# Gated linear attention with a soft mixture of experts: four batches side by side, half blocks through the state, the carry on TensorE, and a new order

## The chip, the core and the metric

The kernel runs on one core of a Trainium2 chip. Five engines run it, each with a queue of its own: TensorE (PE, matrix products, with weight loads listed as PEld), VectorE (DVE), ScalarE (ACT), GpSimd (POOL) and SyncE (SP), which here issues DMAs. Products land in PSUM, eight banks of 512 fp32 values on each of 128 partitions; everything else works in SBUF. The metric is the device time of the program in microseconds.

## The reference

Inputs are q, k, v, a_re, a_im of 4 batches, 8 heads, 768 tokens and 48 channels; a_re is uniform on 0.85 to 0.95, a_im normal with standard deviation 0.1. The attention is a complex decay of a state; its result is the input of a soft mixture of 8 experts with 4 slots each.

```python
mag = np.sqrt(a_re * a_re + a_im * a_im)
scale = np.minimum(mag, 0.999) / (mag + 1e-06)
a_re_n, a_im_n = (a_re * scale, a_im * scale)
for t in range(S):
    new_re = ar * S_re - ai * S_im
    new_im = ar * S_im + ai * S_re
    S_re, S_im = (new_re + kv, new_im)
    y[:, :, t] = np.einsum('bhd,bhde->bhe', q[:, :, t], S_re)
x = y.transpose(0, 2, 1, 3).reshape(B * S, H * D)
logits = x @ phi
d = softmax over tokens of logits; slot_input = d.T @ x
h = np.maximum(slot_input[e] @ w1[e], 0.0); slot_out[e] = h @ w2[e]
out = softmax over slots of logits @ slot_out
```

## The kernel before

Tokens are taken in blocks of 128 (`g`), 24 of them, batch after batch: a block's state comes from the block before it of the same batch. Three blocks form a unit `u`; there are eight units. `_polar` is the fast path. For a group of blocks `gates` takes the logarithm of the decay's size and the ratio a_im/a_re, and `arctan` its angle. `phase` sums angles along the tokens with a triangular product on PE (`up`); the sum so far of the batch is added to one row of the block beforehand on VectorE (L640), then the sum is rounded to whole turns and the rest kept (L646, L648), and sine and cosine are taken on ScalarE (L653, L658). `expo` does the same for the decay (`lp`) and copies the block's last row into `rrow` with DMAs that ScalarE issues (L679); `decay` turns those rows. `mults` multiplies q and k by the decay on GpSimd (L694) and by sine and cosine on VectorE (L703), which gives `hat`; `xpose` turns it (PE L715, ScalarE L718), `score` forms the 128x128 scores of a head and masks them (PE L723, VectorE L727), `attend` adds scores times v and the state's part into `yb` (L748, L750), `delta` carries the state on (PE L761, VectorE L766, L768), and `xform` turns the result back (L773, copied by ScalarE, L776). `_Moe.logits` and `slots` take a unit's three blocks into running softmax sums, `merge` ends these, `hidden` and `experts` apply the weights, and `combine` forms the results of a block at a time and scales them with `rc`.

The order of all this is written out by hand in `ORDER`: each name runs a task's next step, and `_InOrder` holds every engine to the order in which the steps were traced. SP's loads stand in it too: seven weight chunks (`w0` to `w6`) at the start, three more along the way, and two groups of them near the end (`w12`, `w11`), where pools are given up (`swap`, `swap_wk`).

In PSUM a pool `ps2` has four buffers for turned tiles, scores and results (tag `tr`) and two for the rest (tag `lu`); `yb` and `db` have one bank each.

The fast path holds only where the decay behaves. `gates` therefore keeps the largest (a_im/a_re)² and the smallest a_re of each group, L908 to L919 compare them and others with bounds, L940 counts the partitions on which all is well, and L942 writes `bad`. After `_polar` the kernel reads it and, where it is over zero, runs `_stepwise`: the recurrence token by token on VectorE, in 48 rounds of 16 tokens, each with loads into single buffers, and the mixture after it, without overlap:

```python
rv = nc.values_load(bad)
with tc.If(rv > 0):
    with ExitStack() as st:
        _stepwise(st, tc, cst, phi_sb, dict(q=q, k=k, v=v, a_re=a_re, a_im=a_im), w1, w2, out)
```

Of the kernel before, what the change touches and what calls it, by code (L numbers as in the profile page):

```python
# [25 lines left out]
UB = 3  # L26
NU = NG // UB
# [21 lines left out]
TAU_MAX = 1.5  # L49
AR_MIN = 33.0 / 64.0  # L50
# [28 lines left out]

class _Moe:  # L80


# [42 lines left out]
    def slots(self, u, xs):  # L125
# [35 lines left out]
        nc.vector.reciprocal(out=self.rc[:, u, :].unsqueeze(2), in_=cs)

    def merge(self):
# [101 lines left out]
    def weights(self, er, us, j):  # L265
# [4 lines left out]
        yield from self.parts(er(us, j), ep, self.low[0])  # L270
# [5 lines left out]
    def combine(self, er, sr, skip, os_tile, out):  # L276

        nc, w = self.nc, out.shape[-1]
        for u in range(NU):
            os_ = os_tile(u)[:, 0 : UB * w].rearrange("p (j d) -> p j d", j=UB)  # L280
            for j in range(UB):
                o = self.ps.tile([P, skip + w], F32, name="o", tag="tr", bufs=NTR)
                nc.tensor.matmul(out=o, lhsT=er(u, j), rhs=sr, start=True, stop=True)  # L283
                if (UB * u + j) % 2:
                    nc.scalar.activation(out=os_[:, j], in_=o[:, skip:], func=AF.Copy, scale=self.rc[:, u, j : j + 1])
                else:
                    nc.vector.tensor_scalar(out=os_[:, j], in0=o[:, skip:], scalar1=self.rc[:, u, j : j + 1], scalar2=None, op0=ALU.mult)
                if u == 0:
                    nc.sync.dma_start(out=out[u][:, j], in_=os_[:, j])
                yield  # L290
            if u:
                nc.sync.dma_start(out=out[u], in_=os_)

# [3 lines left out]
    L0 lq0 w0 la0 w1 w2 w3 w4 w5 lv0 w6 g0 g0 wu1 g0 g0 wu2 g0 wu0 g0 wu3 g0 g1 g0 g0 g1 e0 g1 e0 g1 e0 e0 m0 T0 g1 t0 t1 p0 p0  # L297
    m0 p0 p0 p1 p0 L1 p1 m0 p1 x2 g1 x0 g1 p2 g1 p2 x0 g1 x2 p2 e1 g2 e2 la1 m0 g2 m0 g2 x1 x3 e1 g2 D0 e1 e1 D0 x1 x3 g2 c0 e2
    e2 c1 T1 c0 m1 c1 a0 e2 p1 a0 t2 p1 p1 p3 p2 p2 p3 m1 p2 L2 m1 x6 x4 p3 m2 x5 x4 x7 x6 d0 x5 d0 D0 x7 lq1 c2 p4 g2 c3 a0 g2
    p4 D1 c2 g2 D1 c3 a1 D1 g2 a1 D1 e3 m2 a1 e3 m2 x8 e3 x10 x8 p4 x9 x10 e3 x9 p5 e4 g3 e5 e4 e4 x11 m3 p5 x11 e4 D2 g3 p5 la2  # L300
    D2 g3 f0 D2 c4 m4 e5 e5 c5 c4 e5 T2 a2 c5 p3 p3 g3 a2 p3 p4 lv1 p4 d1 g3 f1 p4 a2 l0 p5 p5 m5 p5 l0 L3 d1 l0 l0 lq2 s0 s0 m3
    s0 g3 m3 f0 f1 g3 x13 x12 x14 s0 g3 x15 D3 x12 D3 g3 x14 x13 D2 x15 e6 m4 c6 e6 m4 e6 c7 e6 c6 x17 c7 x18 x17 D3 x16 m6 g4
    a3 x16 x18 a3 g4 D3 m5 e7 g4 x19 m5 e8 x19 g4 D4 a3 e7 D4 e7 e7 c8 g4 e8 e8 e8 c9 T3 c8 x22 c9 m7 t3 x21 D4 x20 x20 p6 x22
    m8 a4 x21 p6 a4 p6 p7 lq3 t4 p6 p7 D4 p6 x23 p7 c10 x23 c11 p8 p7 a4 p7 c10 p8 p7 c11 a5 la3 p8 a5 p9 m6 lv2 a5 m6 p8 x24
    x26 x24 p8 x25 m7 x26 x27 p8 l1 m7 L4 p9 l1 x25 D5 p9 x27 D5 g4 d2 c12 g4 c13 x29 d2 p10 g4 x28 p10 x28 g4 x29 c12 e9 p10
    x30 a6 x30 D5 e9 e10 p11 e9 c13 e9 e10 m8 e10 a6 e10 p11 m8 a6 e11 p11 m9 x31 la4 f2 x31 g5 D6 f2 D6 m10 g5 s0 f3 s0 g5 c14
    s0 f3 c15 c14 e11 e11 x32 c15 e11 T4 x33 D6 x34 D6 a7 x32 g5 x34 a7 p9 x33 p9 g5 p9 x35 D7 x35 m9 D7 t5 l1 m9 a7 p12 p10 p10
    l1 f4 m11 p10 f5 f4 p12 d3 f5 c16 d3 D7 p12 lq4 c17 p11 p11 c16 p11 x36 c17 L5 x37 p13 x38 a8 m10 s1 x36 s1 m10 s1 x38 a8
    x37 s1 D7 lv3 s1 a8 g5 p13 s1 l2 g5 x39 D8 x39 l2 s1 g5 D8 p13 c18 c19 c18 x40 c19 x42 x40 g5 x41 x42 x43 x41 x43 m11 e12
    e13 m11 e12 e12 a9 D8 e12 e13 D8 e13 a9 e13 p14 g6 p14 m12 a9 e14 p14 g6 D9 la5 D9 m13 g6 l2 l2 c20 s2 x44 s2 c20 c21 x44 D9  # L310
    e14 x46 c21 a10 x46 D9 e14 g6 T5 s2 a10 g6 e14 x45 x47 x45 s2 f6 x47 p12 f7 p12 m14 d4 f8 f6 d4 f7 c22 a10 t6 c23 c22 lq5
    p13 p13 a11 c23 p13 p15 f8 a11 m12 p14 p14 lv4 s2 m12 p14 x48 L6 s2 x50 s2 x49 m13 p15 x48 x50 x51 m13 x49 D10 x51 p15 D10
    a11 g6 l3 c24 g6 c25 l3 g6 c24 x54 x52 c25 x53 x52 g6 a12 x54 a12 D10 e15 a12 m14 x55 e15 e16 m14 e15 e15 x53 e17 p16 x55 g7
    D11 e16 e16 D11 e16 m15 p16 g7 D11 c26 g7 c27 c26 m16 e17 x58 e17 c27 x57 T6 a13 g7 e17 p15 a13 p15 g7 p15 x56 a13 l3 D12
    x56 l3 m17 x58 D12 t7 p16 x59 f9 p16 p16 lq6 d5 p16 d5 p17 f9 m15 x57 p17 x59 p18 m15 la6 f10 p18 f11 f10 f12 f11 p17 c28
    p18 f12 c29 p17 p17 c28 p17 x62 p19 L7 x61 c29 x60 D11 p19 s3 x63 x60 s3 D12 s3 x62 a14 s3 x61 D12 x63 m16 a14 m16 lv5 D13
    a14 p19 g7 D13 s3 g7 l4 c30 s3 g7 l4 s3 x64 c31 g7 x64 x66 c30 e18 x66 c31 x65 D13 e19 x65 m17 x67 a15 m17 x67 e18 D13 e18
    a15 e18 p20 p18 g8 p20 a15 e19 D14 e19 m18 p20 D14 e19 g8 e20 D14 g8 l4 l4 c32 w7 m19 c33 s4 e20 s4 c32 x69 e20 c33 T7 s4
    x68 s4 x70 g8 p18 a16 x69 x68 g8 a16 x70 e20 p19 x71 p19 m18 f13 p19 f14 x71 m18 c34 f13 f14 m20 a16 x72 c34 c35 x72 p20 x74
    p20 w8 s4 x74 p20 x73 s4 x75 L8 s4 d6 D15 d6 c35 x73 D15 D14 x75 a17 D15 g8 a17 g8 lv6 f15 m19 f16 g8 c36 m19 f15 c37 a17 g8  # L320
    f16 x77 x78 x77 c36 e21 c37 x76 a18 x76 m20 a18 x78 m20 D16 a18 e21 D16 e21 e21 e22 D16 e23 D16 e22 e22 x79 l5 x79 m21 e22
    e23 D17 l5 e23 T8 D17 l5 l5 f17 m22 e23 f18 t8 c38 f17 c39 f18 c38 m23 x80 c39 x82 x80 x81 x82 a19 x81 p21 a19 p21 a19 D17
    x83 p21 d7 x83 f19 c40 d7 p22 p21 f19 p21 c41 p21 c40 a20 c41 m21 a20 m21 x86 a20 D17 x85 x84 p22 x84 x87 x86 p22 l6 p22 p22
    D18 l6 p22 p23 D18 x85 m22 x87 p23 m22 l6 c42 w9 c43 c42 x90 c43 x88 l6 x89 x88 x91 x90 D18 a21 x89 p23 x91 a21 D18 p23 p23
# [701 lines left out]
```

## Time and profile before

| what | value |
|---|---|
| median of 3 runs | 354.81 us (354.74 to 355.31) |
| span of the profiled execution | 354.7 us |
| granted TensorE clock, mean | 0.906 |
| bytes moved by DMA | 54.85 MB |
| read from HBM, written | 49.53 MB, 4.72 MB |

The profile is of one execution. Its page gives the busy time of each engine, the span in 40 slices, and the chain of work that ended last; groups of instructions are listed by line, with tile names as `out<-in`, counts, total and mean duration, and the idle time before them with what ended it. An fp32 product appears as two records, and so as two weight loads; a turn (transpose) as one. Ends of products are modelled, so that starts are the better measure of PE's pace.

### The profile page before, as it was taken

What the parts mean: (1) busy time and instruction counts of PE and PEld (TensorE: products, weight loads), DVE (VectorE), ACT (ScalarE), POOL (GpSimd) and SP (SyncE); (2) the same over time, 40 slices, a digit from 0 to 9 for tenths busy, and PEclk for the clock granted to TensorE, in tenths of its full rate; (3) what the DMA queues carried; (4) which work ended last, traced back from release to release, by engine and by line L of the source; (5) the groups of instructions that cost most, each with busy time, mean ns of one, the idle gap of its engine ahead of it and who ended that gap; (6) DMA issues with size and microseconds to landing.
All of it is one profiled execution on the core that took longest, in us unless ns stands there. A gap on an engine that the chain in (4) does not pass through costs nothing.

```text
span 354.7 us, 6884 instructions
## 1 busy us (share of the span) xinstructions
PE 301.5 (85%) x2758; PEld 229.2 (65%) x2758; DVE 244.9 (69%) x461; ACT 211.0 (59%) x373; POOL 46.6 (13%) x30
## 2 busy tenths in 40 slices
PE   3467498589789979999999799969999999899972
PEld 1135386478577668778778688749788976425551
DVE  3387877889497895898897899748557765504551
ACT  3656567767656776566968676856664645300451
POOL 0000404202400420033005100410230002000000
PEclk9858899969899985999999899969999999789985
DMA  7999612700350330213400720332000389379583
GB/s 264 421 420 419 246 81 71 258 9 1 135 188 13 136 111 23 69 20 140 178 2 1 266 71 1 122 118 68 3 0 2 120 354 409 145 284 421 200 290 105
DMA packets 15287, 54.85 MB, mean 155 GB/s; under 512 B 1936, under 2 KB 8976, under 8 KB 10640
## 3 DMA queue, kind: packets, MB, share of 16 engines
q1 hardware_dynamic: 14480, 54.25, 40.7%
q8 instruction: 24, 0.39, 0.4%
q10 hardware_dynamic: 768, 0.08, 0.2%
q14 instruction: 15, 0.12, 0.1%
HBM read 49.53 MB, written 4.72 MB: 153 GB/s over the span
## 4 chain that ended last, share of the span: by engine, by line
PE 54%; DVE 20%; ACT 12%; issue 4%; DMA 4%; ACTq 3%; SPq 1%; DVEq 0%
PE sp L723 10%; PE tp L715 8%; PE up L643 5%; PE db L761 4%; PE hp L230 4%; PE yb L748 3%; PE op L250 3%; ACTq L679 3%; DVE scT L727 3%; DVE hat L703 3%; PE xp L773 3%; PE yb L750 3%; PE o L283 3%; PE lg L103 2%; DVE n L656 2%
## 5 line engine op out<-in xcount | busy, mean ns | idle before, releaser
L718 ACT COPY hT<-tp 96x512 f32<-96x512 f32 x96 | 51.7, 582 | 35.4 <-PE tp L715 31.9
L694 POOL TENSOR_TENSOR ee<-ee,qkt 128x768 f32<-128x768 f32 x23 | 43.8, 1905 | 216.0 <-DMA rrow<-ee 130.9
L715 PE MATMUL tp<-cst,hat 128*96 128x128 f32 x384 | 58.3, 298 | 11.2 <-DVE hat L703 7.6
L715 PEld LDWEIGHTS tp<-cst,hat 128*96 128x96 f32 x384 | 47.2, 138 | 24.6 <-issue 12.7
L723 PE MATMUL sp<-hT,hT 96*128 96x128 f32 x384 | 51.3, 287 | 1.8 <-ACT xs L776 1.0
L723 PEld LDWEIGHTS sp<-hT,hT 96*128 96x128 f32 x384 | 48.0, 201 | 3.5 <-ACT xs L776 1.2
L703 DVE TENSOR_TENSOR hat<-ee,cs 128x768 f32<-128x768 f32 x48 | 47.2, 1018 | 2.8 <-issue 1.4
L727 DVE TENSOR_TENSOR scT<-sp,cst 128x512 f32<-128x512 f32 x48 | 32.4, 686 | 15.3 <-PE sp L723 15.3
L643 PE MATMUL up<-aat,cst 128*128 128x384 f32 x48 | 24.8, 605 | 17.1 <-ACT aat L632 9.1
L748 PE MATMUL yb<-scT,vt 128*48 128x128 f32 x384 | 37.5, 282 | 1.3 <-DVE scT L727 1.0
L750 PE MATMUL yb<-hT,st 96*48 96x128 f32 x320 | 32.0, 278 | 0.0
L761 PEld LDWEIGHTS db<-vt,hat 128*96 128x96 f32 x320 | 29.7, 166 | 3.0 <-issue 1.9
L761 PE MATMUL db<-vt,hat 128*96 128x48 f32 x320 | 30.2, 248 | 0.0
L748 PEld LDWEIGHTS yb<-scT,vt 128*48 128x48 f32 x384 | 21.1, 124 | 8.2 <-issue 3.4
L643 PEld LDWEIGHTS up<-aat,cst 128*128 128x128 f32 x48 | 8.3, 215 | 22.6 <-ACT aat L632 10.2
L667 PE MATMUL lp<-aat,cst 128*128 128x384 f32 x48 | 21.4, 545 | 1.8 <-DVE aat L625 1.3
L646 DVE TENSOR_SCALAR n<-up 128x384 f32<-128x384 f32 x24 | 13.2, 550 | 13.9 <-PE up L643 13.9
L753 ACT COPY yT<-yb 128x512 f32<-128x512 f32 x24 | 14.0, 583 | 13.2 <-PE yb L750 10.9
L750 PEld LDWEIGHTS yb<-hT,st 96*48 96x48 f32 x320 | 19.7, 126 | 0.0
L658 ACT ACTIVATE cs<-n,kb 128x384 f32<-128x384 f32 x24 | 14.7, 611 | 6.7 <-DVE n L656 6.6
L623 ACT ACTIVATE gt<-aat,kb 128x1152 f32<-128x1152 f32 (+2 forms) x9 | 10.4, 1150 | 10.5 <-DVE aat L621 10.5
L671 ACT ACTIVATE ee<-lp 128x384 f32<-128x384 f32 x24 | 11.7, 488 | 7.7 <-issue 3.1
(133 smaller groups left out, 462.3 us busy)
## 6 DMA issues: line engine op xcount, KB each, us to landing
qkt<-in_qk_dram SPq DMA_DIRECT2D x7, 1152.0 KB
aat<-in_aa_dram SPq DMA_DIRECT2D x7, 1152.0 KB
wx<-in_w_dram SPq DMA_DIRECT2D x7, 1024.0 KB
wx<-in_w_dram SPq DMA_DIRECT2D x5, 1152.0 KB
vt<-in_vv_dram SPq DMA_DIRECT2D x8, 576.0 KB
out_dram<-os SPq DMA_DIRECT2D x7, 384.0 KB
we<-in_w_dram SPq DMA_DIRECT2D x2, 1152.0 KB
wt<-in_w_dram SPq DMA_DIRECT2D x2, 1152.0 KB
```

The costliest lines, as they stand in the source:

```text
L643: PE.matmul(out=up, lhsT=tri_u[par], rhs=ph, start=True, stop=True)
L658: ACT.activation(out=t[:, :, 0, :], in_=a.rearrange("p (h d) -> p h d", d=D), func=AF.Sin, scale=-TWO_PI, bias=kb[:, 2:3])
L667: PE.matmul(out=lp, lhsT=tri_l[par], rhs=aat[u][:, 0, j], start=True, stop=True)
L694: POOL.tensor_tensor(out=e, in0=e, in1=qkt[u][:, j], op=ALU.mult)
L703: DVE.tensor_tensor(out=x, in0=e[:, w].rearrange("p (h d) -> p h d", d=D).unsqueeze(2).broadcast_to([P, H, 2, D]), in1=cs[g], op=ALU.mult,)
L715: PE.transpose(out=tp[:, a, :], in_=hat[g][w][:, 4 * hh + a].rearrange("p c d -> p (c d)"), identity=ident)
L718: ACT.copy(out=hT[g, hh, w], in_=tp)
L723: PE.matmul(out=sp[:, a, :], lhsT=hT[g, hh, 1][:, a, :], rhs=hT[g, hh, 0][:, a, :], start=True, stop=True)
L727: DVE.tensor_tensor(out=t, in0=sp, in1=mask[g % 2].unsqueeze(1).broadcast_to([P, 4, P]), op=ALU.mult)
L748: PE.matmul(out=o, lhsT=vt[u][:, j, h, :], rhs=scT[g, hh][:, a, :], start=True, stop=first)
L750: PE.matmul(out=o, lhsT=st[g - 1][:, h, :], rhs=hT[g, hh, 0][:, a, :], start=False, stop=True)
L761: PE.matmul(out=db[:, h, :], lhsT=hat[g][1][:, h].rearrange("p c d -> p (c d)"), rhs=vt[u][:, j, h, :], start=True, stop=True)
```

## The change

- A unit is now a block of each of the four batches (`UB = 4`, six units), and batches go in pairs: the second pair lags one block behind in the loads of a_re and a_im. Sine, cosine and the product of q and k with the decay are taken for a pair at once. That product is VectorE's; GpSimd has none.
- `gates` has no clamp; the square of the ratio is ScalarE's, with a sum in the place of the maximum, and the guard has other bounds.
- `phase`: the carry is one more product with one row of weights, into the same sum; ScalarE rounds.
- `score`, `delta` and `attend` work on halves of 64 tokens: a block's scores are two 64x64 squares a head, the state is carried in two steps (`stm` after the first half), and the second half reads the state after the first.
- `rrow`'s DMAs are issued by SP, `xs` is copied by VectorE, all PSUM tiles but `yb` and `db` (two banks each now) share the four buffers `tr`.
- Results: the product is turned over, so that columns of the result lie on partitions; three groups of 128 columns, and 18 DMAs of 256 KB. `rc` goes into the weights of the slots instead.
- Weights: chunks of 2,048 columns, three loaded on the way, nine and five where pools are given up, and seven more into freed places.
- `ORDER` is new, and the four products at the start that only kept PE busy are gone.

```diff
-UB = 3
+UB = B
-GROUPS = [(0, 0, 1), (0, 1, UB)] + [(u, 0, UB) for u in range(1, NU)]
+PAIRS = [(u - p, p) for u in range(NST) for p in (1, 0) if 0 <= u - p < NBLK]
+GROUPS = [(0, 0, 1), (0, 1, 2)] + [(u, 0, UB) for u in range(1, NBLK)] + [(NBLK, 2, UB)]
-TAU_MAX = 1.5
-AR_MIN = 33.0 / 64.0
+T2_MAX = 64.0
+E_MAX = 8e-3
+TINY = 2.0**-60
...
     def gates(x):
-        DVE.tensor_scalar(out=t, in0=ar, scalar1=AR_MIN, scalar2=None, op0=ALU.max, op1=ALU.min, accum_out=amin[:, x : x + 1])
-        ACT.activation(out=ar, in_=t, func=AF.Ln)
-        ACT.activation(out=t, in_=ar, func=AF.Exp, scale=-1.0)
-        DVE.tensor_tensor(out=ai, in0=ai, in1=t, op=ALU.mult)
-        DVE.tensor_tensor_reduce(out=t, in0=ai, in1=ai, scale=1.0, scalar=0.0, op0=ALU.mult, op1=ALU.max, accum_out=tmax[:, x : x + 1])
+        ACT.activation(out=r, in_=r, func=AF.Ln, bias=kb[:, 3:4])
+        ACT.activation(out=t, in_=r, func=AF.Exp, scale=-1.0)
+        DVE.tensor_tensor(out=i, in0=i, in1=t, op=ALU.mult)
+        ACT.activation(out=t, in_=i, func=AF.Square, accum_out=tsum[:, x : x + 1])
...
+        ACT.activation(out=t, in_=r, func=AF.Exp, scale=-0.5, bias=kb[:, 1:2], accum_out=esum[:, x : x + 1])
...
+    def phase(s, b):
+        PE.matmul(out=up, lhsT=tri_u[par], rhs=ai[s + p][:, b], start=True, stop=s == 0)
+        if s:
+            r = slice(LAST[par], LAST[par] + 1)
+            PE.matmul(out=up, lhsT=neg[r], rhs=fr[s - 1, p][r, par], start=False, stop=True)
+        ACT.activation(out=n, in_=up, func=AF.Identity, bias=kb[:, 4:5])
...
-            ACT.dma_start(out=rrow[u][j : j + 1, :, c, :], in_=e[r : r + 1, 0].rearrange("p (h d) -> p h d", d=D))
+            SP.dma_start(out=rrow[s, p][par : par + 1, :, c, :], in_=e[r : r + 1, 0].rearrange("p (h d) -> p h d", d=D))
...
+    def mults(s, p):
+        DVE.tensor_tensor(out=qkt[s, p], in0=ee[s, p], in1=qkt[s, p], op=ALU.mult)
-            POOL.tensor_tensor(out=e, in0=e, in1=qkt[u][:, j], op=ALU.mult)
...
+    def score(s, b):
+        sp = tr([P, H, 64], "sp")
+        for h in range(H):
+            for x in range(2):
+                r = slice(64 * x, 64 * x + 64)
+                PE.matmul(out=sp[r, h], lhsT=hT[s, b, 1, h // 4][:, h % 4, r], rhs=hT[s, b, 0, h // 4][:, h % 4, r], start=True, stop=True)
...
+    def delta(s, b):
+                PE.matmul(
+                    out=db[:, x, D * h : D * h + D],
+                    lhsT=hat[s, b][r, 1, h].rearrange("p c d -> p (c d)"),
+                    rhs=vt[s, b // 2][r, b % 2, h, :],
...
+        if s:
+            DVE.tensor_tensor(out=m, in0=d[0], in1=st[s - 1, b], op=ALU.add)
+        DVE.tensor_tensor(out=t, in0=d[1], in1=m, op=ALU.add)
+        DVE.tensor_tensor(out=t, in0=t, in1=rt[:, s, b].unsqueeze(2).broadcast_to([96, H, D]), op=ALU.mult)
...
+    def attend(s, b):
+        for c in range(4):
+            for k in range(2):
+                for x in range(2):
+                    for a in range(2):
+                        h = 2 * c + a
+                        r = slice(64 * x, 64 * x + 64)
+                        o = yb[64 * a : 64 * a + D, x, 64 * c : 64 * c + 64]
+                        if k == 0:
+                            PE.matmul(out=o, lhsT=vt[s, b // 2][r, b % 2, h, :], rhs=scT[s, b][r, h], start=True, stop=s == 0 and x == 0)
+                        elif s or x:
+                            PE.matmul(out=o, lhsT=(sm[s, b] if x else st[s - 1, b])[:, h, :], rhs=hT[s, b, 0, h // 4][:, h % 4, r], start=False, stop=True)
...
+    def combine(self, er, sr, os_tile, out):
+        for n in range(NER):
+            o = self.ps.tile([XW, UB, P], F32, name="o", tag="tr", bufs=NTR)
+            nc.tensor.matmul(out=o, lhsT=sr, rhs=er[n], start=True, stop=True)
...
-    DVE.tensor_reduce(out=t1[:, 0:1], in_=tmax, axis=AX.X, op=ALU.max)
-    DVE.tensor_reduce(out=t1[:, 1:2], in_=amin, axis=AX.X, op=ALU.min)
+    DVE.tensor_reduce(out=t1[:, 0:1], in_=tsum, axis=AX.X, op=ALU.add)
+    DVE.tensor_reduce(out=t1[:, 1:2], in_=esum, axis=AX.X, op=ALU.max)
...
-    DVE.tensor_scalar(out=good[:, 0:1], in0=t1[:, 0:1], scalar1=TAU_MAX * TAU_MAX, scalar2=None, op0=ALU.is_le)
-    DVE.tensor_scalar(out=good[:, 1:2], in0=t1[:, 1:2], scalar1=AR_MIN, scalar2=None, op0=ALU.is_gt)
+    DVE.tensor_scalar(out=good[:, 0:1], in0=t1[:, 0:1], scalar1=T2_MAX, scalar2=None, op0=ALU.is_le)
+    DVE.tensor_scalar(out=good[:, 1:2], in0=t1[:, 1:2], scalar1=E_MAX, scalar2=None, op0=ALU.is_le)
```

More of the change, by code (lines that the diff above doesn't have):

```diff
@@ L274, in outputs @@
             pass
[L276 to L292, printed above, removed]
@@ L296 @@
-ORDER = """
[L297 to L324, printed above, removed]
-    p23 D19 L9 m23 D19 c44 m23 w12 s5 x92 s6 s5 c44 s5 c45 a21 s5 x92 s6 D19 s6 s5 a22 s5 s6 s5 x94 c45 x93 x94 D19 a22 x93 x95
-    c46 x95 a22 c47 c46 a23 c47 a23 f20 f21 f20 s6 a23 f21 l7 s6 f22 l7 s6 f23 f22 l7 l7 s7 me0 f23 w11 w10 er0 s7 me0 s7 er0
-    er2 s7 er0 s7 er2 er7 er2 er1 er7 er7 s7 er8 ze0 er1 me0 er3 me0 s7 me0 er8 er6 me0 me0 er8 er6 me0 er3 er1 si0 er4 si0 er3
-    er5 er6 er5 er4 er4 er5
@@ L573, in load_first @@
[L573 to L583 removed]
+        ar[u] = io.tile([P, UB, HD], F32, name="ar", bufs=1)
@@ L876, in _polar @@
-    for x in range(4):
-        at("wu", warm, x)
+    at("wk", swap_wk)
+    at("we", swap)
     load_first()
@@ L933, in _polar @@
[L933 to L944 removed]
+    moe.outputs(sr[:, 0:XW], op[0])
@@ new lines, in mixture, with os_tile @@
+    def mixture(x):
+        return moe.combine(er, sr[:, XW * x : XW * x + XW], os_tile, out[x])
+    def os_tile(n):
+        n = late["os"]
+        late["os"] += 1
+        if n % 4 == 0:
+            late["ot"] = late["we"].tile([P, 4, UB, P], F32, name=f"we{late['nx']}")
+            late["nx"] += 1
+        return late["ot"][0:XW, n % 4]
+    late["os"] = 0
+    for x in range(NX):
+        nxt = exp[x + 1] if x + 1 < NX else iter(())
+        for _ in range(4):
+            next(nxt, None)
+        for _ in mixture(x):
+            next(nxt, None)
+            next(nxt, None)
+        for _ in nxt:
+            pass
+        if x + 1 < NX:
+            moe.outputs(sr[:, XW * (x + 1) : XW * (x + 2)], op[x + 1])
+        if x == 0:
+            gp = tr([1, 1], "gp")
+            PE.matmul(out=gp, lhsT=t1[:, 0:1], rhs=ones, start=True, stop=True)
+            DVE.tensor_scalar(out=t1[0:1, 1:2], in0=gp, scalar1=P - 0.5, scalar2=None, op0=ALU.is_lt)
+            DVE.tensor_copy(out=bad, in_=t1[0:1, 1:2])
```

633 lines of the change are left out of this document (313 added, 320 removed).

## The prediction

> **What bounds the kernel now.** First the page's busy times, slices and shares of the chain that ended last, then the view of stages.
>
> ```profile
> PE 301.5 (85%) x2758; PEld 229.2 (65%) x2758; DVE 244.9 (69%) x461; ACT 211.0 (59%) x373; POOL 46.6 (13%) x30
> PEclk9858899969899985999999899969999999789985
> PE 54%; DVE 20%; ACT 12%; issue 4%; DMA 4%; ACTq 3%; SPq 1%; DVEq 0%
> 45.00:294.00 249.00, 226.78 (x2174) 188.82 (x2173) 191.99 (x336) 166.79 (x292) 40.43 (x22) 0.94 0.26 93
> 294.00:308.00 14.00, 12.80 (x80) 7.36 (x78) 8.87 (x33) 6.64 (x17) 1.98 (x3) 0.90 0.76 307
> 308.00:355.00 47.00, 37.45 (x411) 19.09 (x410) 16.09 (x47) 12.77 (x30) 0.00 (x0) 0.83 0.67 245
> ```
>
> TensorE is busy 85% of the span and holds 54% of the chain; VectorE and ScalarE follow, none far behind. Attention runs from about 45 us to 294 us. There PE shows 226.8 of 249 us, so what one block of 128 tokens costs on PE comes first and how long the vector engines let it wait second. The last 61 us (294 to 355) are the soft mixture: weights, hidden layer, experts, results. How PE is paced shows in its order of time:
>
> ```profile
> 185.57 1.48 PE L761 MATMUL db<-vt,hat 128*96 128x48 f32 x16
> 188.37 1.95 PE L723 MATMUL sp<-hT,hT 96*128 96x128 f32 x16
> 190.16 1.04 PE L715 MATMUL tp<-cst,hat 128*96 128x128 f32 x8
> 191.12 0.42 PE L748 MATMUL yb<-scT,vt 128*48 128x128 f32 x4
> 191.38 0.39 PE L750 MATMUL yb<-hT,st 96*48 96x128 f32 x4
> 191.60 0.39 PE L748 MATMUL yb<-scT,vt 128*48 128x128 f32 x4
> ```
>
> Sixteen score records take 190.16 − 188.37 = 1.79 us, 0.112 each. Eight transposes take 0.96 us up to the first `yb`; their own 1.04 us holds about 0.27 for the last one to end, so they start 0.11 apart and would need 0.87: the **change of tile shape** (128 weight columns to 48) costs 0.09. Four `yb` records follow every 0.22, 0.055 each: 48-wide outputs in two column halves run side by side.
>
> But one line near the end decides more than all of these:
>
> ```profile
> L617 DVE CUSTOM_DVE_ANT_0 gt<-aat 128x1152 f32<-128x1152 f32 (+2 forms) x9 | 12.5, 1389 | 0.2
> L908 DVE TENSOR_REDUCE good<-tmax 128x1 f32<-128x9 f32 x1 | 0.2, 152 | 0.0
> L942 DVE CAST bad<-good 1x1 int32<-1x1 f32 x1 | 0.1, 142 | 0.0
> L130 ACT ACTIVATION_READ_ACCUMULATOR ls<-ls,nm 96x1 f32 x8 | 1.5, 187 | 0.0
> ```
>
> L617 takes (a_im/a_re)² and its **maximum** for each partition, L908 the maximum over the nine groups, and L942 writes `bad`, which stays 0 here: no instruction of `_stepwise` is in the trace. That function recomputes everything token by token when a guard fails.
>
> **The change, part by part: the guard.** `gates` now squares a_im/a_re on ScalarE with `accum_out=tsum`, a sum over the group; the end adds the eight groups' sums (`op=ALU.add`) and asks for at most T2_MAX = 64. Eight groups are 24 blocks of 384 values, 9,216 a partition. a_im is normal with 0.1, so its square averages 0.01; a_re is uniform on 0.85 to 0.95, so 1/a_re² averages 1/(0.85·0.95) = 1.238. The sum is 9,216 · 0.01238 = **114**, the same on each partition within a few per cent. 114 is not at most 64. Then `good` is 0, `gp` is 0 < 127.5, `bad` is 1, and `_stepwise` runs. (The largest ratio squared is 0.28, so the old bound 2.25 held; the new `esum` test passes: 1,536 · 2e-6/0.9 = 3.4e-3 against 8e-3.) The last row above shows the accumulator being read, of 96x128 tiles only; what it holds for 1,536 elements no row shows. The Trainium skill, "ScalarE activation tables: per-element evaluation and per-set limits", section "What a function is on this engine", says that the accumulator output adds the results along the free dimension; by it the sum is 114 and the stepwise loop runs. If it held only the last 384 of each group, the sum would be 8 · 4.75 = 38 and the guard would pass.
>
> **The stepwise loop.** No row shows it; its operations are like these:
>
> ```profile
> L699 DVE TENSOR_TENSOR ee<-ee,qkt 128x384 f32<-128x384 f32 x2 | 1.1, 556 | 0.0
> 20.42 0.96 DVE L703 TENSOR_TENSOR hat<-ee,cs 128x768 f32<-128x768 f32 x1
> L914 DVE TENSOR_REDUCE good<-goodz 128x1 f32<-128x384 f32 x2 | 1.1, 554 | 0.1
> 17.79 0.56 DVE L646 TENSOR_SCALAR n<-up 128x384 f32<-128x384 f32 x1 [3.89 <-PE up L643]
> 18.39 0.56 DVE L648 TENSOR_TENSOR f<-up,n 128x384 f32<-128x384 f32 x1
> 0.75 0.69 SPq L576 DMA_DIRECT2D aat<-in_aa_dram  x1
> 4.54 0.55 DVE L609 TENSOR_SCALAR_CACHE_REDUCE gt<-aat 128x384 f32<-128x384 f32 x1 [3.01 <-DMA aat<-in_aa_dram]
> ```
>
> An fp32 product of 384 elements takes 0.556 us, of 768 undisturbed 0.96: 1.05 ns an element and 0.15. A token is nine such operations on 128x(48·12) = 576 elements, 0.76 each, and a reduction (0.554 for 384, so 0.75): 7.6; half of them need the one before (17.79 to 18.39 is 0.60 for an operation of 0.56), so 7.7 us. 768 tokens: 5,914 us. Each of the 48 rounds of 16 tokens first loads 20 pieces through SP into single buffers: issues of 0.35 to 0.69 us and 3 us from issue to use (0.75 to 4.54) make about 12; nine operations of 768 elements add 8, the store and the loop's turn some 4 (no row; 0 to 10): 24 · 48 = 1,150. Then the mixture again, unpipelined: 24 loads and transposes of about 5 us, six units, 25 MB of weights at the rate shown below: 280. Loop and all: 7,340. Bounds: 5,750 + 400 + 150 = 6,300 with every load hidden; 5,914 + 1,536 + 1,725 + 450 = 9,625 if each of the 7,680 operations waits 0.2 longer and the extras are half as much again.
>
> **The fast path**, which runs in either case and ends with the guard. TensorE, with counts from these rows and from the code:
>
> ```profile
> 184.08 1.65 PE L667 MATMUL lp<-aat,cst 128*128 128x384 f32 x4
> L723 PE MATMUL sp<-hT,hT 96*128 96x128 f32 x384 | 51.3, 287 | 1.8 <-ACT xs L776 1.0 <-ACT hT L718 0.8
> L748 PE MATMUL yb<-scT,vt 128*48 128x128 f32 x384 | 37.5, 282 | 1.3 <-DVE scT L727 1.0 <-ACT ee L671 0.3
> L750 PE MATMUL yb<-hT,st 96*48 96x128 f32 x320 | 32.0, 278 | 0.0
> L761 PE MATMUL db<-vt,hat 128*96 128x48 f32 x320 | 30.2, 248 | 0.0
> ```
>
> Scores: 384 records at 0.112 are 43 us; now 768 of half the columns (0.056) in two column halves (0.028): 21.5, **−21**. `yb`: 704 at 0.055 are 39; now 704 from the state at 0.028 and 768 over half the rows in four tiles at 0.014, 30: **−8**. `db`: 320 records, 1.48 us for 16 with 0.2 of it the last one's end, 0.085 each, 27; now 704, in two row halves 0.042: **+3**; one after another 59. The phase's carry leaves VectorE for a one-row product of 384 columns: `lp`'s four records take 1.49 us up to `db`, so two cost 0.75, in 20 blocks **+15**. Six units of the mixture in place of eight: −3. Changes of tile shape: counted along the two written orders 106 become 367, of them 192 within `attend`, which goes from half rows to full rows and back four times a call: 261 · 0.09 = **+23**. Together +9 on 225. The Trainium skill, "TensorEngine Tiling (Array Packing)", "Tiling Modes", says that changing the mode drains the engine; our rows agree with 0.09 for columns, and by the rule half rows pay too; were they free, the sum would be −8.
>
> VectorE and ScalarE:
>
> ```profile
> L727 DVE TENSOR_TENSOR scT<-sp,cst 128x512 f32<-128x512 f32 x48 | 32.4, 686 | 15.3 <-PE sp L723 15.3
> L694 POOL TENSOR_TENSOR ee<-ee,qkt 128x768 f32<-128x768 f32 x23 | 43.8, 1905 | 216.0 <-DMA rrow<-ee 130.9 <-ACT aat L632 37.3 <-ACT hT L718 20.6
> L646 DVE TENSOR_SCALAR n<-up 128x384 f32<-128x384 f32 x24 | 13.2, 550 | 13.9 <-PE up L643 13.9
> L640 DVE SCALAR_TENSOR_TENSOR aat<-f,aat 1x384 f32<-1x384 f32 x20 | 10.9, 545 | 1.5 <-ACT aat L632 1.1
> L609 DVE TENSOR_SCALAR_CACHE_REDUCE gt<-aat 128x1152 f32<-128x1152 f32 (+2 forms) x9 | 10.9, 1209 | 3.6 <-DMA aat<-in_aa_dram 3.6
> L766 DVE TENSOR_TENSOR st<-db,st 96x384 f32<-96x384 f32 x16 | 8.8, 548 | 3.7 <-PE yb L750 2.5 <-PE db L761 1.2
> L768 DVE TENSOR_TENSOR st<-st,rt 96x384 f32<-96x384 f32 x16 | 9.4, 587 | 0.1
> L776 ACT COPY xs<-xp 128x384 f32<-128x384 f32 x24 | 11.0, 474 | 8.3 <-PE xp L773 8.3
> L679 ACTq DMA_DIRECT2D rrow<-ee x48: 621/622/1232, 12.3 to 256.6; - x48
> L552 ACT ACT_TABLE_LOAD x10 | 12.8, 1283 | 0.9 <-PEq L1011 0.8
> L555 ACT ACT_TABLE_LOAD x9 | 11.5, 1283 | 4.5 <-ACT ee L673 2.9 <-issue 1.6
> ```
>
> VectorE loses half of the masks (L727, −16), the carry (L640, −11), the rounding (L646, −13), clamp and square (L609 −11, L617 −13); it gains the products (12 of 1,536 elements, 1.8 each by L694's and L703's sizes, +21), the states (64 additions of 0.55 for 36, +15) and `xs` (+13); pooled absolute values, fewer units and larger result copies give some −10, an estimate: about −25. ScalarE loses 48 issues of 0.62 (−30) and `xs` (−11); it gains the rounding (24 like L776's, +11), the squares (L617's elements, +12) and eight table loads (L552, L555: 19 become 27, +10): −8. The issues go to SP's queue; the loads behind them wait with them where a buffer is late, and the decay that needs them comes a block later, so at nothing, or one load's delay. All PSUM work shares four buffers where six were; a product that waits for one holds all of PE's queue. Bound: between 0 and twice the 18 us of stalls that PE has now (249 − 216 of its own paces − 15 for the clock at 0.94). I take no more stalls for it, and −10 for the relieved engines. In the first 45 us the pair puts two blocks through instead of one: −6 (−10 to +4).
>
> The end:
>
> ```profile
> GB/s 18 323 423 411 439 435 414 358 410 420 414 364 31 14 0 0 108 399 425 425 425 435 420 429 394 249 23 161 254 327 338 327 343 167 273 114 221 130 14 5
> ```
>
> Weights arrive at 411 to 439 GB/s at best. Twenty-one chunks of 1.05 MB now come after `swap` (3 are loaded before, where 7 were at the very start and 14 by 294 us); with 4.7 MB of results 26.7 MB, 64 us, of which 3 to 9 chunks can come before attention ends: 42 to 57 us remain, against 61 now. I take −9 (−14 to +2).
>
> Sum for the fast path: 354.7 (the execution's span; the median shown is 354.81) − 6 + 9 − 10 − 9 = **339**.
>
> **Forecast:** 339 + 7,340 = 7,679, about **7,680**; its own range is 6,500 to 10,000.
>
> **Rivals.** (1) The guard passes, because the accumulator holds less than the whole sum: 339, faster; it decides at a sum of 64. For it: the row L130 shows small tiles only. Against it: the softmax's denominators are such sums. (2) The guard passes and vector engines were the true limit: −10 more from stalls, −5 in the tail, 324. (3) The guard passes, but row halves run one after another: `db` +30, `yb` +11 on an engine that already sets the pace: 380, slower; it decides from about 16 us of the 41.
>
> **Chances.** Stepwise loop 0.75; (1) 0.13; (2) 0.06; (3) 0.06. Within (1), whose range is 328 to 358, 0.11 are faster and 0.02 are no change (within 0.2%, about what measurements of this kernel can tell). So faster 0.17, same 0.02, slower 0.81. The range takes in the rivals (1) but for their best and most of the loop's bounds: 330 to 10,000.
>
> **What would show it.** A span of thousands of us with lines of `_stepwise`, about 7,680 VectorE operations of 576 elements at 0.75 us, PE idle meanwhile. If instead the span is some 340 us and ends at the results, the reading of the guard was wrong. In the first 300 us: sixteen `sp` records in about 0.45 us, `db` at 0.04 or 0.085 each, 0.09 at each change inside `attend`, POOL without products, and weights streaming for 40 us and more behind attention.

## The result and the profile after

| | median of 4 runs | lowest to highest |
|---|---|---|
| before | 354.77 us | 353.51 to 355.31 |
| after | 7,879.85 us | 7,876.32 to 7,889.58 |

The changed kernel takes **22.22 times** as long (95% interval 22.09 to 22.35). The forecast was 7,680, with 6,500 to 10,000 as that case's own range (330 to 10,000 over all cases). Of the executions below some are slower by a few per cent at a lower clock (four of e1's seven, and e2's one has their time): the ratios leave them out, the medians do not.

The page of the changed kernel shows at its head the span and the busy times, then the granted clock in 40 slices:

```profile
span 7874.2 us, 28955 instructions
PE 414.8 (5%) x5334; PEld 271.8 (3%) x5334; DVE 6407.3 (81%) x8657; ACT 344.6 (4%) x504; POOL 5.2 (0%) x10
PEclk9855555555555555555555555555555555555556
```

VectorE is busy 81% of the span and TensorE 5%. The costliest groups come next (operation, tiles and count, then busy time in all and mean ns of one, then idle time ahead and what ended it):

```profile
L397 DVE TENSOR_REDUCE s_y<-s_c 128x12 f32<-128x576 f32 x768 | 875.4, 1140 | 1.7
L395 DVE TENSOR_TENSOR sr<-s_a,s_b 128x576 f32<-128x576 f32 x768 | 582.3, 758 | 26.5
L388 DVE TENSOR_TENSOR s_a<-sr,s_a_re 128x576 f32<-128x576 f32 x768 | 577.0, 751 | 0.0
L371 DVE TENSOR_TENSOR s_mg<-s_a_re 128x768 f32<-128x768 f32 x48 | 46.0, 959 | 973.6 <-DMA s_a_re<-in_a_re_dram 973.6
L376 DVE RECIPROCAL s_t<-s_t 128x768 f32<-128x768 f32 x48 | 237.8, 4953 | 1.7
L375 DVE TENSOR_SCALAR s_t<-s_mg 128x768 f32<-128x768 f32 x48 | 26.9, 561 | 108.1 <-ACT s_mg L374 108.1
```

All lie in `_stepwise`: 768 times a line for its 768 tokens, 48 times for its 48 rounds. Where the loop takes over shows in the order of time:

```profile
324.66 0.14 DVE L952 CAST bad<-good 1x1 int32<-1x1 f32 x1
...
335.15 1.97 DVE L284 COPY we<-o 128x512 f32<-128x512 f32 x3 [0.59 <-PE o L279]
337.60 0.54 DVE L357 MEMSET sr<- 128x576 f32 x1 [0.48 <-DVE we L284]
```

L952 writes `bad`; 10 us later VectorE copies out the last results, and its next instruction, L357, clears the loop's state. The view of stages divides the span (length of the stretch, busy time of PE, weight loads, DVE, ACT and POOL with instructions, clock, DMA share, GB/s):

```profile
45.00:294.00 249.00, 244.01 (x3730) 179.97 (x3728) 174.33 (x291) 178.00 (x285) 2.52 (x3) 0.97 0.32 111
294.00:341.00 47.00, 34.77 (x509) 17.67 (x508) 13.09 (x36) 7.47 (x14) 0.00 (x0) 0.94 1.02 412
341.00:355.00 14.00, 0.00 (x0) 0.00 (x0) 0.48 (x1) 0.00 (x0) 0.00 (x0) 0.50 0.77 213
355.00:7665.00 7310.00, 0.00 (x0) 0.00 (x0) 6128.59 (x8112) 102.00 (x96) 0.00 (x0) 0.50 0.05 11
7665.00:7874.00 209.00, 109.54 (x894) 57.51 (x894) 69.08 (x188) 19.06 (x51) 2.52 (x3) 0.63 0.48 162
```

The first 341 us are the fast path, whose results the loop computes anew. Fourteen us pass with the branch and the first loads; the loop takes 7,310, and the second mixture 209. In 45 to 294 TensorE is now busy 244 of 249 us, where it was 227.

### The profile page after: what moved, and what is told of

It reads as the page before. It is cut to its first block, busy times and chain, and to the rows that moved or that the text cites. A ratio compares the mean times of both kernels' runs of the same rounds, so it can differ in the third digit from the quotient of the medians.

```text
span 7874.2 us, 28955 instructions
## 1 busy us (share of the span) xinstructions
PE 414.8 (5%) x5334; PEld 271.8 (3%) x5334; DVE 6407.3 (81%) x8657; ACT 344.6 (4%) x504; POOL 5.2 (0%) x10
## 5 line engine op out<-in xcount | busy, mean ns | idle before, releaser
L397 DVE TENSOR_REDUCE s_y<-s_c 128x12 f32<-128x576 f32 x768 | 875.4, 1140 | 1.7
L371 DVE TENSOR_TENSOR s_mg<-s_a_re 128x768 f32<-128x768 f32 x48 | 46.0, 959 | 973.6 <-DMA s_a_re<-in_a_re_dram 973.6
L395 DVE TENSOR_TENSOR sr<-s_a,s_b 128x576 f32<-128x576 f32 x768 | 582.3, 758 | 26.5
L396 DVE TENSOR_TENSOR s_c<-sr,s_q 128x576 f32<-128x576 f32 x768 | 582.2, 758 | 26.7
L394 DVE TENSOR_TENSOR s_b<-s_k,s_v 128x576 f32<-128x576 f32 x768 | 577.5, 752 | 0.0
L392 DVE TENSOR_TENSOR si<-s_c,s_e 128x576 f32<-128x576 f32 x768 | 577.2, 752 | 0.0
L391 DVE TENSOR_TENSOR s_e<-sr,s_a_im 128x576 f32<-128x576 f32 x768 | 577.1, 751 | 0.0
L390 DVE TENSOR_TENSOR s_c<-si,s_a_re 128x576 f32<-128x576 f32 x768 | 577.0, 751 | 0.0
L393 DVE TENSOR_TENSOR s_a<-s_a,s_b 128x576 f32<-128x576 f32 x768 | 577.0, 751 | 0.0
L388 DVE TENSOR_TENSOR s_a<-sr,s_a_re 128x576 f32<-128x576 f32 x768 | 577.0, 751 | 0.0
L389 DVE TENSOR_TENSOR s_b<-si,s_a_im 128x576 f32<-128x576 f32 x768 | 574.8, 748 | 0.0
L376 DVE RECIPROCAL s_t<-s_t 128x768 f32<-128x768 f32 x48 | 237.8, 4953 | 1.7
L375 DVE TENSOR_SCALAR s_t<-s_mg 128x768 f32<-128x768 f32 x48 | 26.9, 561 | 108.1 <-ACT s_mg L374 108.1
```

The lines of the kernel that those rows point to most:

```text
L376: DVE.reciprocal(out=t2, in_=t2)
L388: DVE.tensor_tensor(out=a, in0=sr, in1=rb, op=ALU.mult)
L389: DVE.tensor_tensor(out=b, in0=si, in1=ib, op=ALU.mult)
L390: DVE.tensor_tensor(out=c, in0=si, in1=rb, op=ALU.mult)
L391: DVE.tensor_tensor(out=e, in0=sr, in1=ib, op=ALU.mult)
L392: DVE.tensor_tensor(out=si, in0=c, in1=e, op=ALU.add)
```

## The experiments

Nine kernels ran in three sets, each set with the kernel before beside it. e4 is built on e1, e5 to e7 on e4 and e8 on e6, so their ratios to before are compared: e1 0.985, e4 0.931, e5 0.934, e6 0.896, e7 0.878, e8 0.900, each with an interval of about ±0.01 or less. A difference of two of them is therefore good to about 4 us. e2, e3 and e9 ran once each.

### Is it the guard, and which part of it?

**e1**, the bound alone:

```diff
-T2_MAX = 64.0
+T2_MAX = 128.0
```

> The changed kernel with the bound of the guard's sum at 128 in place of 64 (the guard's meaning changes, no product does). Theory (only the guard makes the kernel slow; the sum over a partition lies near 114, so between 64 and 128): the loop does not run, and what is left is the fast path. The forecast gave it 339 us (328 to 358). The trace of the changed kernel, which also runs this path first, has its last result issued at 340.8, and before has 5.7 us from there to the end of its span: 346.5, ratio 0.977. Rival (3), row halves of TensorE one after another: 380. Rival (2), the vector engines were the limit: 324. If another of the five tests fails, or the sum is above 128: about 7,880 again.

Measured: 0.985 of before (0.978 to 0.992), the three runs that it rests on at 348.7 to 349.4 with spans of 346.5 to 347.2. The loop is gone, so the sum lies between 64 and 128, as the 114 worked out from the inputs says. The time is that read from the changed kernel's trace (346.5), not the forecast's 339.

**e2**, the joining of the groups alone:

```diff
-    DVE.tensor_reduce(out=t1[:, 0:1], in_=tsum, axis=AX.X, op=ALU.add)
+    DVE.tensor_reduce(out=t1[:, 0:1], in_=tsum, axis=AX.X, op=ALU.max)
```

> The changed kernel with one word changed in the guard: the eight groups' sums of squares are joined by their maximum in place of their sum, the bound stays at 64 (the guard's meaning changes, no product does). Theory (it is the total over groups that is too large: the largest group holds 4 batches x 384 = 1,536 of 9,216 elements, so 1,536 x 0.01238 = 19, well below 64): the guard passes, about 346.5 us as with a bound of 128. Rival (the accumulator of a single Square already goes over the bound, or another test of the five fails): about 7,880.

Measured: 364.83 us in its one run, no loop (before in this set: 353 to 360). No group exceeds 64, their total does, and no other of the five tests fails. The Trainium skill's statement that the accumulator output adds the results along the free dimension ("ScalarE activation tables: per-element evaluation and per-set limits", "What a function is on this engine") agrees: the guard fails at 64 and passes at 128.

**e3**, the old guard made to fail in the old kernel:

```diff
-TAU_MAX = 1.5
+TAU_MAX = 0.125
```

> The kernel before with its own guard made to fail: the bound of the largest |a_im/a_re| at 0.125 in place of 1.5 (its square 0.0156, where the guard of before looks at the largest square of all elements, which is more than their mean of 0.0124 by far). Theory (the time is the fast path plus the loop, and the loop is the same text in both kernels): SyncE takes the branch at 350.0 in before and at 342.0 in the changed kernel, whose span goes on for 7,532 us from there; so about 350 + 7,532 = 7,882 us, within 20 of the changed kernel's 7,880. Rival (something of the change itself slows the loop, its buffers or its order): clearly less, by hundreds of us.

Measured: 7,897.65 us, 18 above the changed kernel. The loop's groups are those shown above:

```profile
span 7895.8 us, 25858 instructions
L408 DVE TENSOR_REDUCE s_y<-s_c 128x12 f32<-128x576 f32 x768 | 875.6, 1140 | 1.7
L406 DVE TENSOR_TENSOR sr<-s_a,s_b 128x576 f32<-128x576 f32 x768 | 582.1, 758 | 26.5
```

So nothing else of the change slows the loop: the whole factor of 22 is the price of a guard that fails, in either kernel. The loop with its mixture is 10 us longer here (7,542 from SyncE's branch at 353.3, against 7,532 from 342.0): from the last token's reduction to the end of the span, which is the second mixture, it is 229 us against 209, with eight units in before and six in the changed kernel, and what lies ahead of it takes 10 less.

### What does a round of the loop cost?

**e9**, eight tokens a round:

```diff
-    T, G, EG = 16, 4, D // 4
+    T, G, EG = 8, 4, D // 4
```

> The changed kernel, bound at 64 as in the change, with the loop in rounds of 8 tokens in place of 16: the same 768 tokens, 96 rounds in place of 48, each with the same 36 loads and stores of half the size. It measures what a round costs beside its tokens. In the trace of the changed kernel a round takes 152.7 us: 16 tokens of 7.33 and 35.4, of which VectorE waits 20.5 for stores and loads and works 14.9 on the tile of decays. Theory (the waiting is paid per piece on SyncE's queue, the work per element): 48 more rounds of 20.5 us, about 980 more, 8,860. Rival (the waiting is paid per byte): no change, 7,880. The forecast's sizes (12 for loads and 4 for the rest, per round) would give 770 more, 8,650.

Measured: 9,040.94 us, 1,161 more. The end of a round of the changed kernel (16 tokens), in order of time:

```profile
486.34 1.15 DVE L397 TENSOR_REDUCE s_y<-s_c 128x12 f32<-128x576 f32 x1
487.51 7.93 SPq L400 DMA_DIRECT2D xd<-s_y  x16
498.25 1.88 SPq L366 DMA_DIRECT2D s_q<-in_q_dram  x4
...
506.46 1.81 SPq L366 DMA_DIRECT2D s_a_im<-in_a_im_dram  x4
508.06 0.96 DVE L371 TENSOR_TENSOR s_mg<-s_a_re 128x768 f32<-128x768 f32 x1 [20.57 <-DMA s_a_re<-in_a_re_dram]
```

and of e9 (8 tokens):

```profile
424.83 1.15 DVE L397 TENSOR_REDUCE s_y<-s_c 128x12 f32<-128x576 f32 x1
426.00 7.93 SPq L400 DMA_DIRECT2D xd<-s_y  x16
436.53 1.89 SPq L366 DMA_DIRECT2D s_q<-in_q_dram  x4
...
444.68 1.81 SPq L366 DMA_DIRECT2D s_a_im<-in_a_im_dram  x4
446.06 0.56 DVE L371 TENSOR_TENSOR s_mg<-s_a_re 128x384 f32<-128x384 f32 x1 [20.09 <-DMA s_a_re<-in_a_re_dram]
```

Sixteen stores take SyncE 7.93 us and twenty loads 10, whatever their size: pieces of half the bytes take the same. VectorE waits 20.5 us from its last reduction to its first product in the one, 19.9 in the other (medians of all rounds). The waits are 96 · 19.9 − 48 · 20.5 = 926 us more, near the 980 expected. Most of the rest was not expected: the work on the tile of decays went from 14.9 us a round to 9.8, not to half, so that 96 · 9.8 − 48 · 14.9 = 226 us come on top; the Sqrt's table load (1.28), which comes again each round, is a part of what did not halve. Together that is 1,152 of the 1,161.

### Where does the fast path's time lie?

**e4**, the order of products in `attend` (with the bound at 128, as in all that follow but e8):

```diff
-        for c in range(4):
-            if c == 2:
+        for k in range(2):
+            if k == 1:
                 yield "a1"
-            for k in range(2):
+            for c in range(4):
...
-                            PE.matmul(out=o, lhsT=vt[s, b // 2][r, b % 2, h, :], rhs=scT[s, b][r, h], start=True, stop=s == 0 and x == 0)
+                            PE.matmul(out=o, lhsT=vt[s, b // 2][r, b % 2, h, :], rhs=scT[s, b][r, h], start=c == 0 or s + x == 0, stop=s + x == 0)
...
-                                stop=True,
+                                stop=c == 3,
```

> The changed kernel with the bound at 128, and attend regrouped: all sixteen products of the scores (half rows), then all sixteen of the states (96 rows), in place of four turns of four and four; the same products, 144 changes of tile shape fewer. Theory (TensorE sets the pace of attention, and a change costs time on it): a product that follows a change starts 146 to 149 ns after the one before it, one that opens a new set of four of the same kind 73 to 87; so 144 x 0.067 = 10 us less than the run with a bound of 128 alone, by the 0.09 of the forecast 13. Rival (TensorE waits for other engines at these places, so the change is hidden): no difference, within 1 us.

Measured: 331.27 us, 0.931 of before (0.923 to 0.939), so 19 less than e1 by the ratios, twice what was expected. First half a call of `attend` in the changed kernel, with the product that follows it, then a whole call in e4 (start, duration, line, tiles, count of records; a product leaves two):

```profile
195.48 0.33 PE L766 MATMUL yb<-scT,vt 64*48 64x64 f32 x8
195.74 0.32 PE L768 MATMUL yb<-hT,st 96*48 96x64 f32 x4
195.89 0.28 PE L768 MATMUL yb<-hT,stm 96*48 96x64 f32 x4
...
196.72 0.85 PE L154 MATMUL sip<-xs,d 128*32 128x384 f32 x8
```

```profile
197.02 0.67 PE L766 MATMUL yb<-scT,vt 64*48 64x64 f32 x32
197.61 0.32 PE L768 MATMUL yb<-hT,st 96*48 96x64 f32 x4
...
198.43 0.28 PE L768 MATMUL yb<-hT,stm 96*48 96x64 f32 x4
198.64 0.64 PE L704 MATMUL tp<-cst,hat 128*96 128x128 f32 x4
```

A half call takes 196.72 − 195.48 = 1.24 us, a whole one 2.48; regrouped it takes 198.64 − 197.02 = 1.62. The 0.86 between, 24 times, are 20.6 us, and with six changes fewer in a call each is worth 0.14. The trace shows where it goes, product by product: in a steady row a set of four (half rows) starts 36 ns after the last record of the set before it, a set of two (96 rows) 49; behind a change the first set comes after 146 to 149, and the second is late too, after 73 to 87. A change therefore costs (146 − 49) + (87 − 49) = 135 or (149 − 36) + (73 − 36) = 150 ns, about **0.14 us**, where the expectation had taken the second set's delay for the normal pace. The Trainium skill ("TensorEngine Tiling (Array Packing)", "Tiling Modes") has changes drain the engine and names no price; the trace agrees that a change delays what follows, by 0.14 us, and half rows pay as columns do.

**e5**, the products on GpSimd:

```diff
-        DVE.tensor_tensor(out=qkt[s, p], in0=ee[s, p], in1=qkt[s, p], op=ALU.mult)
+        (POOL if (s, p) != PAIRS[0] else DVE).tensor_tensor(out=qkt[s, p], in0=ee[s, p], in1=qkt[s, p], op=ALU.mult)
```

> The regrouped kernel (e4) with the products of decay and queries or keys on GpSimd again for all pairs but the first, as in before; no GpSimd products was one part of the change. In e4 TensorE is busy 41 to 45 of each 45 us from 45 to 270 and VectorE 30 to 36, so the theory (TensorE sets the pace) says: VectorE loses 11 products of 1.75 us, and nothing comes of it: within 3 us of e4's 331. Rival (2) of the forecast (a vector engine is the limit): 10 us or more faster. Rival (GpSimd's product, 1.9 us for 768 elements in before, so 3.8 here, holds up hats and the transposes behind them): 4 us or more slower.

Measured: 332.63 us, 0.934 (0.925 to 0.943): no difference from e4. Its groups show what is traded:

```profile
L683 POOL TENSOR_TENSOR qkt<-ee,qkt 128x1536 f32<-128x1536 f32 x11 | 41.7, 3802 | 201.0 <-ACT ee L665 201.0
L692 DVE TENSOR_TENSOR hat<-qkt,cs 128x1536 f32<-128x1536 f32 x24 | 46.1, 1928 | 4.6 <-ACT cs L650 3.4 <-POOL qkt L683 1.1
```

VectorE loses eleven products of 1.75 us, 19 in all; `hat` grows on the same VectorE from 1.75 (e4: 1,748 ns) to 1.93 beside GpSimd, 4 in all. Neither reaches the end of the kernel, and rival (2) is out; that TensorE sets the pace, e4 and e7 show directly.

**e6**, the buffers of the weights in another order:

```diff
+    WE = [4, 5, 6, 7, 8, 0, 1, 2, 3]
...
-        for x in range(BUF["we"]):
-            wload(we, name=f"we{x}")
+        t = [we.tile([P, WC], F32, name=f"we{x}") for x in range(BUF["we"])]
+        for x in WE:
+            wload(we, t=t[x])
```

(the later uses of these buffers follow the same list)

> The regrouped kernel (e4) with the nine weight chunks that follow the swap loaded in another order of their buffers: 4, 5, 6, 7, 8, 0, 1, 2, 3; the same chunks in the same sequence. In e4 the third load waits on SyncE's queue from 247.3 to 260.0, since buffer 2 lies where values of the last block are still read; the six behind it, whose buffers lie over gates, decays and phases, wait with it, and the chip's memory moves 2 to 60 GB/s in that time. Theory (the end is set by the weights' arrival at 420 GB/s): 12.7 us of loading come earlier, about 13 us less than e4's 331, so 318 (315 to 321). Rival (the tail is set by TensorE's products and the results behind them): less than 4 us gained.

Measured: 316.29 us, 0.896 (0.891 to 0.901), so 12.5 less than e4 by the ratios. SyncE's queue in e4 in order of time (start, length of the group, count of issues), and the stretches around it:

```profile
246.52 17.73 SPq L595 DMA_DIRECT2D we<-in_w_dram  x9
```

```profile
230.00:246.50 16.50, 16.50 (x279) 13.43 (x279) 13.09 (x22) 12.90 (x23) 0.00 (x0) 1.00 0.01 2
246.50:260.00 13.50, 13.50 (x321) 11.67 (x322) 5.54 (x13) 5.72 (x13) 2.52 (x3) 1.00 0.43 158
275.00:322.00 47.00, 35.14 (x504) 17.91 (x496) 11.49 (x31) 7.46 (x14) 0.00 (x0) 0.92 0.98 396
```

and in e6:

```profile
233.51 25.47 SPq L597 DMA_DIRECT2D we<-in_w_dram  x9
```

```profile
237.60:247.00 9.40, 9.40 (x160) 7.71 (x163) 6.94 (x11) 6.32 (x13) 0.00 (x0) 1.00 1.01 419
272.00:307.00 35.00, 31.02 (x508) 16.56 (x500) 11.49 (x31) 7.46 (x14) 0.00 (x0) 0.99 0.98 390
```

The last two columns are the ones to read. In e4 the nine issues are spread over 17.7 us: two at 246.5, seven from 260.0 on. Memory moves 2 GB/s before the first two and 158 on the mean up to 260 (the two chunks; the expectation's 2 to 60 was misread), and is full (0.98) from 275 on. In e6 five chunks are issued from 233.5 to 238.1, two at 244, and the last two, into buffers 2 and 3, at 257.5. Memory moves 419 GB/s from 237.6, while attention still runs, and the stretch of the hidden layer, experts and results, 47 us in e4, is 35 us, with PE busy 31 of them. The weights' arrival set the end, and what held it was a load that waits for its buffer at the head of an in-order queue: first that into buffer 0, then that into buffer 2. The size came out by another count than the expectation's, though: e6 waits for buffer 2 too, from 244.9 to 257.5, but by then seven chunks are through where e4 had two, and five chunks of 1.05 MB at 419 GB/s are 12.5 us.

**e7**, no carry:

```diff
-        PE.matmul(out=up, lhsT=tri_u[par], rhs=ai[s + p][:, b], start=True, stop=s == 0)
-        if s:
-            r = slice(LAST[par], LAST[par] + 1)
-            PE.matmul(out=up, lhsT=neg[r], rhs=fr[s - 1, p][r, par], start=False, stop=True)
+        PE.matmul(out=up, lhsT=tri_u[par], rhs=ai[s + p][:, b], start=True, stop=True)
```

> The regrouped kernel (e4) without the carry: the 40 one-row products that bring the phase's last row over from the block before are left out, so the phases lack what earlier blocks add. Theory (the carry is TensorE's own time on the pace): 40 records of 0.42 us, so about 17 us less than e4's 331, 314; the forecast priced it at 15. Rival (it is hidden: TensorE would wait there for other engines): under 5 us less.

Measured: 310.86 us, 0.878 (0.868 to 0.887): 19 less than e4 by the ratios. The carry (20 products, of which the trace holds two records each, the 40 of the expectation) is paid in full: 20 · 0.84 = 16.8 us on TensorE by the rows below. The phase's two products in the changed kernel, first that of 128 rows, then the carry of one:

```profile
193.80 0.91 PE L629 MATMUL up<-ai,cst 128*128 128x384 f32 x2
194.64 0.91 PE L632 MATMUL up<-f,cst 1*128 1x384 f32 x2
```

The second starts 0.84 us behind the first, and the next row in this order, L766 shown above, at 195.48, 0.84 behind the second: one row costs TensorE as much as 128.

**e8**, the old guard on the fastest version:

```diff
-T2_MAX = 128.0
+T2_MAX = 2.25
...
-        ACT.activation(out=t, in_=i, func=AF.Square, accum_out=tsum[:, x : x + 1])
+        DVE.tensor_tensor_reduce(out=t, in0=i, in1=i, scale=1.0, scalar=0.0, op0=ALU.mult, op1=ALU.max, accum_out=tsum[:, x : x + 1])
...
-    DVE.tensor_reduce(out=t1[:, 0:1], in_=tsum, axis=AX.X, op=ALU.add)
+    DVE.tensor_reduce(out=t1[:, 0:1], in_=tsum, axis=AX.X, op=ALU.max)
```

> e6 with the guard of before: squares and their largest value by one VectorE instruction for each of the eight groups, in place of ScalarE's Square with its running sum; largest value at most 2.25, joined by maximum over the groups. This brings the guard's old meaning back. Theory (TensorE and, at the end, the weights set the time): VectorE takes about 10 us more work and ScalarE 10 less, beside TensorE: within 2 us of e6. Rival (VectorE has no room left): 5 us or more slower than e6.

Measured: 318.80 us, 0.900 (0.892 to 0.908), against 0.896 for e6; the intervals overlap. The sum bought nothing that can be measured. This version keeps the old guard's bound on the ratio (the other tests are the changed kernel's) and is 10% faster than before.

## Why the prediction was right, step by step

**The guard** was read rightly, and everything hung on it: e1 and e2 show that the total over groups is what fails, e3 that the loop alone makes the time. Rival (1), an accumulator holding less than the whole sum, is out; so is rival (2) by e5, and rival (3): in the changed kernel's trace the `db` records start 78 and 7 ns apart by turns, two for 85, which is two row halves side by side, and e1 is at 0.985, not 380 us.

**The loop** was forecast at 7,340 and took 7,533 (from 341 to 7,874), by three errors that partly cancel, so that its nearness is in part luck:

| term | forecast | measured | difference |
|---|---|---|---|
| 768 tokens | 7.7 us each, 5,914 | 7.33 each, 5,632 | −282 |
| 48 rounds beside their tokens | 24 each, 1,150 | 35.4 each, 1,700 | +550 |
| second mixture | 280 | 209 | −71 |

What makes a token cheaper than the sum of its operations shows in the order of time:

```profile
370.16 0.75 DVE L388 TENSOR_TENSOR s_a<-sr,s_a_re 128x576 f32<-128x576 f32 x1
370.83 0.75 DVE L389 TENSOR_TENSOR s_b<-si,s_a_im 128x576 f32<-128x576 f32 x1
...
374.18 0.75 DVE L394 TENSOR_TENSOR s_b<-s_k,s_v 128x576 f32<-128x576 f32 x1
374.96 0.76 DVE L395 TENSOR_TENSOR sr<-s_a,s_b 128x576 f32<-128x576 f32 x1
...
376.43 0.75 DVE L388 TENSOR_TENSOR s_a<-sr,s_a_re 128x576 f32<-128x576 f32 x1
377.10 1.14 DVE L397 TENSOR_REDUCE s_y<-s_c 128x12 f32<-128x576 f32 x1
```

An operation of 0.75 us is followed after 0.67 by the next, and after 0.78 where the next reads what it has just written (L394, L395). Nine take 376.43 − 370.16 = 6.27, where the forecast added 0.76 each. The last two rows show the next token's first product ahead of the reduction, which takes 1.14 rather than the 0.75 worked out from L914; that it reads its tile across, as L914 does not, may be why, and wasn't tried. The rounds were mis-sized by more: of the 35.4 us, 20.5 are the wait for stores and loads, forecast at 12 with 4 for store and turn, and 14.9 the work on the decays, forecast at 8. There the forecast counted nine operations alike and missed that RECIPROCAL (L376) takes 4.95 us where a product of the same tile (L371) takes 0.96, and that VectorE waits 108.1/48 = 2.3 us a round for ScalarE's root (L375).

**The fast path** was forecast at 339 and takes 346.5 to 347.2 in e1. Each product's start measured from the one before it, put down to the later one, without the excess over 0.45 us of gaps longer than 1 us, gives TensorE's own time up to the first product of the hidden layer:

| us | before | after | difference | forecast |
|---|---|---|---|---|
| scores `sp` | 47.6 | 27.9 | −19.7 | −21 |
| `yb` | 45.9 | 61.8 | +15.9 | −8, and +17 for its 192 changes of shape |
| `db` | 29.5 | 40.0 | +10.5 | +3 |
| `up` and `lp`, with the carry | 36.3 | 50.4 | +14.1 | +15 |
| transposes `tp` | 57.9 | 51.9 | −6.0 | 0 |
| the rest | 52.4 | 40.2 | −12.2 | −3, and +6 for other changes |
| sum | 269.6 | 272.2 | +2.6 | +9 |
| waits, first product's start | 38.5 | 22.3 | −16.2 | −16 (head −6, stalls −10) |
| hidden layer begins at | 308.0 | 294.5 | −13.5 | −7 |

Scores, carry and stalls came as forecast; e7 puts the carry at 19 give or take 4, against 15. Two sizes were off. In `yb` a change of tile shape costs 0.14 and not 0.09 (e4). `db` keeps the forecast 85 ns for two records in a steady call, but two of its 24 calls ran at about 150, in stretches with a granted clock of 0.50 (26 to 30 us) and 0.60 (48 to 51); that is 2 us of its excess, and what makes the rest stays open. The rest and `tp` gained 18 where +3 was forecast; a part of it may be the clock, granted at 0.97 in 45 to 294 after and at 0.94 before, and how much wasn't tried.

**The tail** is the step of the fast path that failed: −9 was forecast, and from the hidden layer's begin to the end of the span it went from 46.7 us (354.7 − 308.0) to 52.0 (346.5, the span of e1's shortest run, less the 294.5 of the changed kernel's trace), +5. The forecast let 3 to 9 of 21 chunks come before attention ends and so 42 to 57 us of loading remain, and took 52. SyncE's queue in the changed kernel, and the stretches around it:

```profile
264.34 20.13 SPq L595 DMA_DIRECT2D we<-in_w_dram  x9
```

```profile
270.00:281.00 11.00, 11.00 (x252) 9.13 (x248) 4.19 (x11) 2.86 (x6) 2.52 (x3) 1.00 0.11 44
281.00:341.00 60.00, 46.80 (x609) 24.70 (x607) 23.87 (x71) 14.19 (x32) 0.00 (x0) 0.95 1.00 403
```

Two of the nine issues go at 264 and the third at 281.0, where the last `yb` products run, so only two chunks came before attention ended; from then on memory is full (1.00) for the 60 us to the last results. What the runs showed in place of the forecast's 3 to 9 is that the queue stood still behind buffer 2 of the swap, which overlies values that the last block still reads; e6 loads five other buffers ahead of it and gains 12.5. The range of the forecast for the fast path, 328 to 358, still held it.

## What to carry to other kernels

Work out each guard's value from the inputs before pricing any stage behind it: one bound can outweigh every other part of a change, and a sum over elements needs another bound than a maximum over them. Where buffers of a late stage overlie those of an early one, load first what lies over the values that die first, since one waiting load holds all that are queued behind it. Group products of one tile shape; a change costs as much as several of the small products between which it lies.

## What the hardware showed unexpectedly

- A change of tile shape delays two sets of products, not one: 146 to 149 ns to the first and 73 to 87 to the second, against 36 to 49 in a steady row.
- RECIPROCAL of 768 fp32 elements takes 4.95 us on VectorE, five times a product of two such tiles.
- VectorE products of 0.75 us start 0.67 apart, and 0.78 apart where the later one reads what the earlier one wrote.
- Twenty loads take SyncE 10.0 us to issue with 16 tokens to a piece and with 8: the loop's loads cost by their number, 0.5 us each.
- The row of the loop's stretch shows a granted clock of 0.50 where TensorE has no product for 7,310 us.
